# Decoding float64 weights inside an expert pass: raw pieces in resident buffers, half-steps spread over four expert slots

## The chip, the cores and the metric

The kernel runs on one core of one Trainium2 chip. The metric is device time in microseconds (us); the kernel before takes 666.78 us, the median of 3 runs (662.82 to 666.97).

## What is computed

Attention with pooled queries feeds a mixture of experts (each token goes to one of 8 experts by the argmax of its gate), and that feeds a dense layer. Only the dense layer's weights come as float64.

```python
q_pool = q.reshape(B, H, S // 2, 2, D).mean(axis=3)
attn = softmax(scale * q_pool @ k.T);  x = attn @ v              # 1152 tokens x 512
e_idx = argmax(x @ w_gate)
for e in range(8):                                                # w1[e] 512x1024, w2[e] 1024x512
    ye = np.maximum(x[e_idx == e] @ w1[e], 0.0) @ w2[e]
    out[e_idx == e] = gate_w * eom * ye
h = out @ w_in;  g = h * tanh(softplus(h));  return g @ w_out     # w_in, w_out float64
```

## The kernel before

There are three stages in a row. Attention and the routing take roughly the first 280 us, the experts run until 437 us, and the dense layer (tiles zps, u, n, l, gh, gl, ops) takes the rest. TensorE multiplies in float32 with operands split in two: an ACT copy makes the high part (names ending in h), a subtraction on DVE or POOL the low part (names ending in l), and three matmuls a product (lines 1012 to 1014).

**The float64 weights.** They are 32 pieces of 128 x 512 numbers. `load_raw` (from line 508) loads the raw 512 KB of a piece into a tile wraw; `decode` (from line 528) turns it into float32 in the resident tiles `wd[0]` to `wd[15]`, two pieces to a tile, in two half-steps. Half-step 0 has `ACT dm<-wraw` (absolute value of the high word, line 91) and on DVE two operations that make ds (sign and low bits, lines 100 and 97). Half-step 1 has three operations on DVE: two on dm (clamp, shift) and one that writes wd. `raw_ahead` keeps at most two pieces loaded that are not decoded. Pieces 0 to 21 are decoded in the attention stage; pieces 22 to 31 in the expert stage, where the load is issued from ACT's queue (line 513), ACT works in order, and an issue waits there until the buffer is free.

**The expert pass.** Eight slots run one after the other, each one expert of a given size. This text numbers them 0 to 7. Wide slots: 0 and 3 (three blocks of 128 tokens) and 5 (two blocks), ten steps each. Narrow slots: 1 (128 tokens) and 2, 4, 6, 7 (64 tokens), six steps each. One counter q runs over all steps: slot 0 has q 0 to 9, slot 1 q 10 to 15, slot 2 q 16 to 21, slot 3 q 22 to 31, slot 4 q 32 to 37, slot 5 q 38 to 47.

In step i of a wide slot, TensorE makes one block of hidden units (hps, for i under 8) and adds hidden block i - 2 to the output (yp). Between the two stand `ACT hh<-hps` and `DVE hl<-hps,hh`; two hps buffers exist, so a block of hps waits for the hl of two blocks before. Weights (tiles wt, 1 MB each, four to an expert, five buffers) are loaded by SP in order as buffers come free; ACT makes w1h and w2h, DVE w2l and the first three w1l, POOL the other w1l. Slot 1 has the same split for its second product; the 64-token slots multiply in plain float32 and need only ACT (hr, hn). The block of tokens of the next wide slot is prepared in the narrow slot before it (xh on ACT, xl on DVE).

**Where decoding stands in the pass.** The loop over q (from line 1271) calls, after the matmuls and splits of a step, as many half-steps as the table DECS gives. Before, the table has a row for each wide slot, and a step counts from q = 8 on:

```python
DECS = [[0] * 8 + [1, 2], [2, 1] * 5, [2] + [0] * 9]    # slots 0, 3, 5: 3, 15 and 2 half-steps
```

At q = 7 the routing's memory on the right side of SBUF is given up (the last DMA from it is `gbuf<-gt`, the gates' 4.5 KB, issued by ACT), the pool `dq` is opened in it (two wraw, two dm, one ds), and the first two raw loads are issued. When piece 31 is decoded (q = 38), the pool is closed, and `split_hi` (ACT wh, 1024 wide) and `split_lo` (DVE wl or wd) of the dense layer's first four weight tiles run in every second step from there on.

Of the kernel before, what the change touches and what calls it, by code (L numbers as in the profile page):

```python
# [9 lines left out]
F32 = mybir.dt.float32  # L10
F32R = mybir.dt.float32r
F16 = mybir.dt.float16
I32 = mybir.dt.int32
# [7 lines left out]
P = 128  # L21
# [63 lines left out]
def kernel(ctx, tc, cst, qt, kt, v, wgo, w1, w2, wio, out):  # L85
# [48 lines left out]
    wd = [cp.tile([P, 1024], F32, name="wd", bufs=16) for f in range(16)]  # L134
# [8 lines left out]
    ap = astack.enter_context(tc.tile_pool(name="ap", bufs=1, side="right"))  # L143
# [38 lines left out]
    DEC_M = 32  # L182
# [39 lines left out]
    KC = 384  # L222
# [280 lines left out]

    dq, wq = [], []
    wraw, dmt, dst_ = {}, {}, {}

    def load_raw(i, pool):
        f, c = divmod(i, 2)
        if pool is ap and i % 2:
            wraw[i] = wd[12].bitcast(I32).rearrange("p (a b) -> p a b", b=2)  # L510
        else:
            wraw[i] = pool.tile([P, 512, 2], I32, name="wraw", bufs=1 if pool is ap else 2)
        (SP if pool is ap else A).dma_start(out=wraw[i].rearrange("p a b -> p (a b)"), in_=wio[f, :, 512 * c:512 * (c + 1)].bitcast(I32))

    def decode_abs(pool, i=None):
        early = i is None
        if early:
            i = dec[0] + (dec[0] in dmt)
        if i not in dmt and i in wraw and now[0] - since.get(i, 0) >= (3 if early else 0):
            m = dmt[i] = pool.tile([P, 512], F32, name="dm", bufs=2)  # L520
            act(m, wraw[i][:, :, 1].bitcast(F32), AF.Abs)

    clamped = set()
# [6 lines left out]
    def decode(i, part, pool):  # L530
        f, c = divmod(i, 2)
        lo, hi = wraw[i][:, :, 0], wraw[i][:, :, 1]
        dst = wd[f][:, 512 * c:512 * (c + 1)]
        decode_abs(pool, i)
        if part == 0:
            s = dst_[i] = wd[15][:, KC:KC + 512].bitcast(I32) if pool is ap else pool.tile([P, 512], I32, name="ds", bufs=1)
            ts(V, s, hi, -0x80000000, ALU.bitwise_and)
            stt(s, lo, 29, s, ALU.logical_shift_right, ALU.bitwise_or)
        else:
            s, m = dst_[i], dmt[i]  # L540
            mi = m.bitcast(I32)
            decode_clamp(V, i)
            ts(V, mi, mi, 3, ALU.logical_shift_left, 0x40000000, ALU.bitwise_xor)
            stt(dst.bitcast(I32), mi, 0x7FFFFFFF, s, ALU.bitwise_and, ALU.bitwise_or)
# [149 lines left out]
    def raw_ahead(pool, end):  # L694
        while dec[2] < min(dec[0] + 2, end):
            load_raw(dec[2], pool)
            since[dec[2]] = now[0]
            dec[2] += 1

    def decode_step(pool, end):  # L700
        if dec[0] >= dec[2]:
            return
        decode(dec[0], dec[1], pool)
        dec[1] += 1
        if dec[1] == 2:
            dec[0], dec[1] = dec[0] + 1, 0
# [515 lines left out]
    NPRE = 4  # L1222
# [19 lines left out]
    LATE = 1  # L1242
    XGB = 4

    DECS = [[0] * 8 + [1, 2], [2, 1] * 5, [2] + [0] * 9]
    RQ = 2
    slots = []
    for pos_ in order:
# [31 lines left out]
    for q, (n_, i, _, main, w_, _) in enumerate(flat):  # L1280
        if i == 0:
            used += len(slots[n_][1])
            if n_ + 1 < len(slots):
                load_w(slots[n_ + 1][0], ej, slots[n_ + 1][0])
        if q + 2 < len(flat):
            flat[q + 2][2]()
        if gnext < min(used + 4, len(allc)):
            gather(*allc[gnext])
            gnext += 1
        for f in xpre.pop(-q - 1, ()):  # L1290
            f()
        main()
        if q + 2 < len(flat):
            flat[q + 2][5]()
        if q == RQ:
            routing_rest()
            over = routing_over()
        if RQ < q <= RQ + 4:
            oi = next(over)
        if q == RQ + 5:  # L1300
            routing_oix(oi)
            T.transpose(pr[:TT, P:2 * P], gsc, ident)
            gt_ = rt("gt", [P])
            act(gt_[:TT], pr[:TT, P:2 * P])
            A.dma_start(out=gbuf.rearrange("(t p) o -> t (p o)", p=P), in_=gt_[:TT])
            rstack.close()
            fstack = ExitStack()
            fp.append(fstack.enter_context(tc.tile_pool(name="fps", bufs=1, space=PSUM, side="right", reuse_waits="tile")))
            dstack = ExitStack()
            dq.append(dstack.enter_context(tc.tile_pool(name="dq", bufs=1, side="right", reuse_waits="tile")))  # L1310
            raw_ahead(dq[0], DEC_M)
        if w_ and q > RQ + 5:
            for _ in range(DECS[slots[n_][0]][i]):
                decode_step(dq[0], DEC_M)
            raw_ahead(dq[0], DEC_M)
        if dec[0] == DEC_M and dq and not wq:
            dstack.close()
            wq.append(ctx.enter_context(tc.tile_pool(name="wq", bufs=1, side="right", reuse_waits="tile")))
            q0 = q
        elif wq and (q - q0) % 2 == 0 and len(ws2) < NPRE:  # L1320
            f = len(ws2)
            split_hi(0, f)
            split_lo(0, f)
# [268 lines left out]
```

## Time and profile before

| | us |
|---|---|
| median of 3 runs (lowest, highest) | 666.78 (662.82, 666.97) |
| the profiled execution's own time | 667.41 |
| its span, first to last instruction | 665.3 |
| TensorE busy in the span | 624.4 |
| VectorE (DVE) busy | 482.9 |
| ScalarE (ACT) busy | 398.8 |
| GpSimd (POOL) busy | 256.5 |

The rows of the trace are from the profiled execution, and their times count from the start of its span. A row of the timeline gives start, duration, engine, line and operation (out<-in), how many were merged, and in brackets how long the engine sat idle before it and what ended that. "L1012" is line 1012 of the kernel before.

### The profile page before, as it was taken

Reading aid. Unit: us, or ns where it says so; the run is one execution under the profiler, and the core shown is the slowest. Engines: PE = TensorE matmul, PEld = TensorE weight load, DVE = VectorE, ACT = ScalarE, POOL = GpSimd, SP = SyncE. Lnnn points to the kernel's source line nnn. Section 1 sums busy time; section 2 is a strip of 40 time slices with the busy share of each in tenths; the row PEclk is TensorE's granted clock in tenths of the full one; section 3 lists DMA queues with packets and bytes.
Section 4 is the critical chain, followed back from the end, with each engine's and each line's share of the span. In section 5 each row is a group of like instructions: output and inputs, shape, how many; then the busy total and the mean of one; then the engine's idle time right before and its main releaser. Section 6 shows DMA issues by size and latency. Waiting matters only on the chain.

```text
span 665.3 us, 11329 instructions
## 1 busy us (share of the span) xinstructions
PE 624.4 (94%) x4122; PEld 502.0 (75%) x4122; DVE 482.9 (73%) x992; ACT 398.8 (60%) x842; POOL 256.5 (39%) x237
## 2 busy tenths in 40 slices
PE   7899999999999999599899989988999999999995
PEld 4667778777777766388669858677888999999993
DVE  4557797978887787566539947229999796888764
ACT  7588888888888664242445464336665544556442
POOL 6555647374656232341215132112222232324221
PEclk8699999999999999699899998989999999999999
DMA  6857564365452231584898795820000110001001
GB/s 242 294 135 230 163 183 123 107 183 170 102 174 63 89 115 52 166 337 156 303 352 287 274 326 186 286 102 0 2 0 1 48 48 1 1 7 42 1 0 53
DMA packets 27410, 89.90 MB, mean 135 GB/s; under 512 B 2886, under 2 KB 7631, under 8 KB 23250
## 3 DMA queue, kind: packets, MB, share of 16 engines
q1 hardware_dynamic: 22320, 75.07, 32.7%
q0 software_dynamic: 3568, 8.79, 5.7%
q10 hardware_dynamic: 1458, 5.25, 2.3%
q8 instruction: 34, 0.56, 0.3%
q14 instruction: 30, 0.25, 0.1%
HBM read 79.65 MB, written 9.97 MB: 135 GB/s over the span
## 4 chain that ended last, share of the span: by engine, by line
PE 36%; DVE 8%; issue 4%; DMA 1%; ACT 1%; POOL 0%; DVEq 0%; ACTq 0%; POOLq 0%
PE ops L1439 10%; PE zps L1013 4%; PE zps L1012 4%; PE zps L1014 4%; PE hps L1162 2%; DVE l L97 2%; DVE n L97 2%; PE yp L1013 2%; PE yp L1012 2%; PE yp L1014 2%; PE yp L1033 2%; PE hps L1012 1%; PE hps L1014 1%; PE hps L1013 1%; DMA wt<-in_w 1%
## 5 line engine op out<-in xcount | busy, mean ns | idle before, releaser
L100 POOL TENSOR_SCALAR u<-u 128x384 f32<-128x384 f32 x48 | 59.7, 1243 | 150.3 <-ACT u L91 121.3
L91 ACT ACTIVATE pt<-sc 128x320 f32<-128x320 f32 (+1 forms) x198 | 87.9, 490 | 12.9 <-PE sc L322 10.2
L341 PE MATMUL pv<-pt,vt 128*64 128x288 f32 x576 | 75.6, 411 | 0.0
L103 DVE TENSOR_REDUCE Mp<-mx 128x1 f32<-128x384 f32 x72 | 40.1, 556 | 42.8 <-PE mx L237 37.7
L324 PE MATMUL sc<-qs,at 128*128 128x320 f32 (+1 forms) x264 | 68.8, 305 | 0.0
L322 PE MATMUL sc<-qb,Bt 66*128 66x320 f32 (+1 forms) x264 | 67.7, 301 | 0.0
L1012 PE MATMUL zps<-yh,wh 128*128 128x384 f32 x188 | 64.4, 342 | 1.7 <-DVE n L97 1.7
L1014 PE MATMUL zps<-yl,wh 128*128 128x384 f32 x188 | 63.6, 338 | 0.0
L1013 PE MATMUL zps<-yh,wd 128*128 128x384 f32 x180 | 61.2, 340 | 0.0
L1439 PE MATMUL ops<-wh,gl 128*128 128x512 f32 x144 | 57.8, 404 | 2.9 <-DVE gl L94 2.4
L341 PEld LDWEIGHTS pv<-pt,vt 128*64 128x64 f32 x576 | 39.0, 137 | 28.5 <-issue 5.2
L1439 PE MATMUL ops<-wh,gh 128*128 128x512 f32 x144 | 56.9, 395 | 0.2 <-ACT gh L91 0.2
L1439 PE MATMUL ops<-wd,gh 128*128 128x512 f32 x135 | 53.3, 395 | 0.0
L100 POOL TENSOR_SCALAR dm<-dm 128x512 f32<-128x512 f32 x21 | 41.5, 1978 | 23.1 <-ACT dm L91 23.0
L94 POOL TENSOR_TENSOR Bt<-kd,at 64x576 fp32r<-64x576 f32 x32 | 46.1, 1452 | 7.1 <-ACT at L91 7.0
L324 PEld LDWEIGHTS sc<-qs,at 128*128 128x128 f32 x264 | 47.4, 194 | 1.3 <-issue 1.0
L322 PEld LDWEIGHTS sc<-qb,Bt 66*128 66x128 f32 x264 | 46.5, 194 | 0.1
L91 ACT ACTIVATE l<-n,two 128x384 f32<-128x384 f32 x48 | 29.5, 615 | 24.9 <-DVE n L97 24.9
L91 ACT ACTIVATE u<-zps 128x384 f32<-128x384 f32 x48 | 23.2, 484 | 33.4 <-PE zps L1014 30.7
L97 DVE SCALAR_TENSOR_TENSOR l<-n,r 128x384 f32<-128x384 f32 x48 | 26.6, 554 | 20.1 <-ACT r L91 20.1
L1012 PEld LDWEIGHTS zps<-yh,wh 128*128 128x128 f32 x188 | 35.6, 190 | 3.7 <-ACT r L91 2.0
L237 PE MATMUL mx<-at,qs 128*128 128x384 f32 x120 | 36.4, 371 | 2.0 <-DVE Mp L103 1.0
(314 smaller groups left out, 1604.9 us busy)
## 6 DMA issues: line engine op xcount, KB each, us to landing
wt<-in_w SPq DMA_DIRECT2D x32, 1024.0 KB, 7.4
kd<-in_kt SPq DMA_DIRECT2D x16, 576.0 KB, 8.2
wraw<-in_wio SPq DMA_DIRECT2D x11, 512.0 KB, 6.1
wd<-in_wio SPq DMA_DIRECT2D x11, 512.0 KB, 4.0
wraw<-in_wio ACTq DMA_DIRECT2D x10, 512.0 KB, 6.0
vt<-in_v SPq DMA_DIRECT2D x8, 576.0 KB, 5.8
tq<-in_qt SPq DMA_DIRECT2D x12, 288.0 KB, 5.5
tq<-in_qt POOLq DMA_DIRECT2D x12, 288.0 KB, 6.8
```

The lines of the kernel that those rows point to most:

```text
L91: A.activation(out=out, in_=in_, func=func, **kw)
L94: eng.tensor_tensor(out=out, in0=a, in1=b, op=op)
L97: V.scalar_tensor_tensor(out=out, in0=a, scalar=s, in1=b, op0=op0, op1=op1)
L100: eng.tensor_scalar(out=out, in0=a, scalar1=s1, scalar2=s2, op0=op0, op1=op1)
L103: V.tensor_reduce(out=out, in_=in_, axis=AX.X, op=op)
L322: mm(o, lhsT=Bt[(2 * p + h) % NBL][:66, ks], rhs=QB[p, h][:66, qs_], start=False, stop=last_, skip_group_check=not (first and last_))
L324: mm(o, lhsT=At[p, h][:, ks], rhs=QS[p, h][:, qs_], start=first, stop=False, skip_group_check=not (first and last_))
L341: mm(pvt[p][f][64 * h:64 * h + 64, :HQ], lhsT=vt[p][:, t, h, :], rhs=Pt[p, t][:, h, f * HQ:(f + 1) * HQ], start=t == 0, stop=t == KT - 1, ...
L1012: mm(out_, lhsT=a, rhs=c, start=first, stop=False)
L1013: mm(out_, lhsT=b_, rhs=c, start=False, stop=False)
L1014: mm(out_, lhsT=a, rhs=d, start=False, stop=last_)
L1439: mm(opt[b_, j], lhsT=(g_, g_, gl_)[i], rhs=(wo, wl_, wo)[i], start=f == 0 and i == 0, stop=f == NF - 1 and i == 2)
```

## The change

Four edits. First, raw loads start at q = 3 instead of q = 7: until the pool is opened, pieces go into `wd[14]` and `wd[15]` (tiles that are decoded last and are free by then), with `wd[13]` for the two work tiles. So pieces 22, 23 and 24 are loaded there. Second, DECS is a table over slots 0 to 3: 5 half-steps in slot 0 (q 5 to 9), 2 in slot 1 (q 14, 15), 3 in slot 2 (q 16 to 18), 10 in slot 3 (one in each step), none in slot 5. Third, the pool `dq` is opened at q = 7 as before, but its first raw load (piece 25) is issued at q = 8. Fourth, `split_hi` and `split_lo` of the first four dense tiles run at q 39, 41, 43 and 45 instead of 40, 42, 44 and 46.

```diff
+    scratch = object()
     def load_raw(i, pool):
         f, c = divmod(i, 2)
-        if pool is ap and i % 2:
+        if pool is scratch:
+            wraw[i] = wd[14 + i % 2].bitcast(I32).rearrange("p (a b) -> p a b", b=2)
+        elif pool is ap and i % 2:
...
-            m = dmt[i] = pool.tile([P, 512], F32, name="dm", bufs=2)
+            m = dmt[i] = wd[13][:, 512:] if pool is scratch else pool.tile([P, 512], F32, name="dm", bufs=2)
...
-            s = dst_[i] = wd[15][:, KC:KC + 512].bitcast(I32) if pool is ap else pool.tile([P, 512], I32, name="ds", bufs=1)
+            if pool is scratch:
+                s = wd[13][:, :512].bitcast(I32)
...
-    DECS = [[0] * 8 + [1, 2], [2, 1] * 5, [2] + [0] * 9]
+    DECS = [[0] * 5 + [1] * 5, [0] * 4 + [1, 1], [1] * 3 + [0] * 3, [1] * 10]
...
-            raw_ahead(dq[0], DEC_M)
-        if w_ and q > RQ + 5:
-            for _ in range(DECS[slots[n_][0]][i]):
-                decode_step(dq[0], DEC_M)
-            raw_ahead(dq[0], DEC_M)
+        if q > RQ and n_ < len(DECS):
+            dp_ = dq[0] if dq else scratch
+            for _ in range(DECS[n_][i]):
+                decode_step(dp_, DEC_M)
+            raw_ahead(dp_, DEC_M)
...
-            q0 = q
-        elif wq and (q - q0) % 2 == 0 and len(ws2) < NPRE:
+        elif wq and n_ == 5 and i % 2 and len(ws2) < NPRE:
```

TensorE's, POOL's and SP's instructions keep their order. ACT's and DVE's move, as the following rows show; "waits" names what an instruction waits for by semaphore, and a DMA's eight semaphores are DMAHW0 to DMAHW7.

ACT, from the gates' store at q = 7 (end of slot 0) to the first relu of slot 1 (hh 128x512), before:

```order
L91 ACTIVATE gt<-pr 9x128 [waits PE_49]
L1305 DMA gbuf<-gt 9x128 [waits Activation_49]
L513 DMA wraw<-in_wio 128x1024 [waits DVE_49] x2
L91 ACTIVATE dm<-wraw 128x512 [waits DMAHW3_49,DMAHW2_49,DVE_49]
L91 ACTIVATE w2h<-wt 128x512 [waits DMAHW7_49]
L91 ACTIVATE w2h<-wt 128x512
L91 ACTIVATE y<-yp 128x512 [waits PE_49] x3
L91 ACTIVATE dm<-wraw 128x512 [waits DMAHW4_49]
L513 DMA wraw<-in_wio 128x1024 [waits DMAHW6_49,DVE_49,Activation_49]
L91 ACTIVATE w2h<-wt 128x512 x2
L91 ACTIVATE hh<-hps 128x512 [waits PE_49]
```

The same place in the changed kernel:

```order
L91 ACTIVATE gt<-pr 9x128 [waits PE_49]
L1314 DMA gbuf<-gt 9x128 [waits DMAHW5_49,Activation_49]
L91 ACTIVATE dm<-wd 128x512 [waits DMAHW1_49]
L516 DMA wraw<-in_wio 128x1024 [waits DMAHW6_49,DMAHW5_49,DVE_49]
L91 ACTIVATE w2h<-wt 128x512 [waits DMAHW0_49]
L91 ACTIVATE w2h<-wt 128x512
L91 ACTIVATE y<-yp 128x512 [waits PE_49] x3
L91 ACTIVATE dm<-wd 128x512 [waits DMAHW3_49]
L91 ACTIVATE w2h<-wt 128x512 x2
L91 ACTIVATE hh<-hps 128x512 [waits PE_49]
```

The two loads and the absolute value that waits for the first of them are gone from this place; what is left is one load (piece 25), which waits for DMAHW5, the semaphore of the gates' store right before it.

DVE, in the first two steps of slot 5 (hl 128x256 is the low part of its hidden blocks), before:

```order
L97 SCALAR_TENSOR_TENSOR hl<-hps,hh 128x256
L94 TENSOR_TENSOR w2l<-wt,w2h 128x512
L100 TENSOR_SCALAR ds<-wraw 128x512
L97 SCALAR_TENSOR_TENSOR ds<-wraw,ds 128x512
L100 TENSOR_SCALAR dm<-dm 128x512 x2
L97 SCALAR_TENSOR_TENSOR wd<-dm,ds 128x512
L97 SCALAR_TENSOR_TENSOR hl<-hps,hh 128x256
L94 TENSOR_TENSOR w2l<-wt,w2h 128x512
```

The same place in the changed kernel:

```order
L97 SCALAR_TENSOR_TENSOR hl<-hps,hh 128x256
L94 TENSOR_TENSOR w2l<-wt,w2h 128x512
L97 SCALAR_TENSOR_TENSOR hl<-hps,hh 128x256
L94 TENSOR_TENSOR w2l<-wt,w2h 128x512
L94 TENSOR_TENSOR wl_4882<-wd,wh 128x1024
```

The five operations of piece 31 no longer stand between the first and the second hl; the first dense split (wl) comes one step earlier.

DVE, from the last splits of slot 1 through slot 2 to the first w1l of slot 3, in the changed kernel:

```order
L94 TENSOR_TENSOR w2l<-wt,w2h 128x512 x2
L100 TENSOR_SCALAR dm<-dm 128x512 x2
L97 SCALAR_TENSOR_TENSOR wd<-dm,ds 128x512
L100 TENSOR_SCALAR ds<-wraw 128x512
L97 SCALAR_TENSOR_TENSOR ds<-wraw,ds 128x512
L100 TENSOR_SCALAR dm<-dm 128x512 x2
L97 SCALAR_TENSOR_TENSOR wd<-dm,ds 128x512
L94 TENSOR_TENSOR xl<-xps,xh 128x4x128
L100 TENSOR_SCALAR ds<-wraw 128x512
L97 SCALAR_TENSOR_TENSOR ds<-wraw,ds 128x512
L94 TENSOR_TENSOR xl<-yb_4295,xh 128x4x128
L100 TENSOR_SCALAR dm<-dm 128x512 x2
```

Before, DVE has there only the splits w2l, the three xl and then w1l; five half-steps (pieces 24 to 26) are new between them.

## Rows read from the trace of the kernel before

**Rows 1.** The page: busy us of each engine over the span.
```profile
PE 624.4 (94%) x4122; PEld 502.0 (75%) x4122; DVE 482.9 (73%) x992; ACT 398.8 (60%) x842; POOL 256.5 (39%) x237
```

**Rows 2.** Stretches: length, busy of PE, PEld, DVE, ACT, POOL, clock, DMA share, GB/s.
```profile
299.00:306.00 7.00, 7.00 (x37) 6.35 (x36) 6.59 (x21) 2.00 (x4) 2.35 (x2) 1.00 0.80 300
306.00:314.00 8.00, 8.00 (x50) 6.87 (x49) 4.75 (x17) 2.62 (x5) 0.00 (x0) 1.00 0.00 0
327.00:350.00 23.00, 21.51 (x128) 14.89 (x129) 9.83 (x17) 10.74 (x23) 6.16 (x6) 0.93 1.00 353
...
329.10:332.50 3.40, 3.40 (x10) 2.26 (x11) 1.55 (x3) 1.74 (x3) 0.77 (x1) 0.51 0.98 402
...
346.50:380.70 34.20, 34.20 (x176) 30.40 (x176) 31.12 (x52) 17.44 (x34) 11.78 (x10) 1.00 0.82 287
...
400.80:404.20 3.40, 3.40 (x15) 3.20 (x15) 3.40 (x6) 0.96 (x3) 0.47 (x1) 0.51 0.29 120
```

**Rows 3.** Timeline of PE in slot 1 and at the start of slot 5.
```profile
317.96 7.30 PE L1201 MATMUL hps<-xn,wt 128*128 128x128 f32 x64
327.19 0.50 PE L1012 MATMUL yp<-w2h,hh 128*128 128x512 f32 x1 [1.93 <-ACT hh L91]
328.99 0.67 PE L1013 MATMUL yp<-w2h,hl 128*128 128x512 f32 x1 [1.30 <-DVE hl L97]
...
400.52 0.39 PE L1012 MATMUL hps<-xh,w1h 128*128 128x256 f32 x1 [3.76 <-DVE hl L97]
```

**Rows 4.** Timeline of ACT, end of slot 0 and start of slot 1.
```profile
314.35 0.55 ACTq L1305 DMA_DIRECT2D gbuf<-gt  x1
314.94 0.98 ACTq L513 DMA_DIRECT2D wraw<-in_wio  x2
321.88 0.69 ACT L91 ACTIVATE dm<-wraw 128x512 f32<-128x512 f32 x1 [7.57 <-DMA wraw<-in_wio]
322.47 1.14 ACT L91 ACTIVATE w2h<-wt 128x512 fp32r<-128x512 f32 x2
...
323.51 1.55 ACT L91 ACTIVATE y<-yp 128x512 f32<-128x512 f32 x3
324.94 0.68 ACT L91 ACTIVATE dm<-wraw 128x512 f32<-128x512 f32 x1
325.51 1.15 ACT L91 ACTIVATE w2h<-wt 128x512 fp32r<-128x512 f32 x2
326.55 0.60 ACT L91 ACTIVATE hh<-hps 128x512 fp32r<-128x512 f32 x1
```

**Rows 5.** Timeline of DVE at the start of slot 5.
```profile
394.83 0.69 DVE L94 TENSOR_TENSOR w2l<-wt,w2h 128x512 fp32r<-128x512 f32 x1 [2.13 <-ACT w2h L91]
395.44 0.42 DVE L100 TENSOR_SCALAR ds<-wraw 128x512 int32<-128x512 int32 x1
...
396.50 2.90 DVE L100 TENSOR_SCALAR dm<-dm 128x512 f32<-128x512 f32 x2
...
400.05 0.42 DVE L97 SCALAR_TENSOR_TENSOR hl<-hps,hh 128x256 fp32r<-128x256 f32 x1
```

**Rows 6.** Timeline of DVE: last hidden block of slot 0.
```profile
311.90 0.56 DVE L97 SCALAR_TENSOR_TENSOR hl<-hps,hh 128x384 fp32r<-128x384 f32 x1 [2.31 <-ACT hh L91]
```

**Rows 7.** Decode operations by tile: count, ns min/median/max, first and last start; landing of raw pieces.
```profile
L100 DVE TENSOR_SCALAR ds<-wraw x10: 414/424/437, 321.8 to 395.4; 128x512 int32<-128x512 int32 x10
L97 DVE SCALAR_TENSOR_TENSOR wd<-dm,ds x10: 691/693/1664, 325.2 to 399.4; 128x512 int32<-128x512 int32 x10
...
DMA to landing us min/median/max: 3.7/6.0/7.0
```

**Rows 8.** Timelines of DVE before slot 3 and of ACT in its first step.
```profile
339.72 0.69 DVE L94 TENSOR_TENSOR xl<-xps,xh 128x512 fp32r<-128x512 f32 x1 [4.70 <-ACT xh L91]
342.70 0.69 DVE L94 TENSOR_TENSOR xl<-yb,xh 128x512 fp32r<-128x512 f32 x1 [2.29 <-ACT xh L91]
...
349.31 0.63 ACT L91 ACTIVATE w2h<-wt 128x512 fp32r<-128x512 f32 x1
```

More of the change, by code (lines that the diff above doesn't have):

```diff
@@ L535, in decode @@
         if part == 0:
-            s = dst_[i] = wd[15][:, KC:KC + 512].bitcast(I32) if pool is ap else pool.tile([P, 512], I32, name="ds", bufs=1)
+            if pool is scratch:
+                s = wd[13][:, :512].bitcast(I32)
+            elif pool is ap:
+                s = wd[15][:, KC:KC + 512].bitcast(I32)
+            else:
+                s = pool.tile([P, 512], I32, name="ds", bufs=1)
+            dst_[i] = s
             ts(V, s, hi, -0x80000000, ALU.bitwise_and)
```

## The prediction

> **What bounds the kernel now.** Read the page first: TensorE is busy for 624.4 us of a span of 665.3, 94% [rows 1]. So a change that adds and removes no matmul can win only TensorE's idle time and the time in which its clock is low. Next, read the expert stage stretch by stretch, because only that stage is touched, and look for TensorE's idle times and the clock. In slot 3, where 15 of the 20 half-steps stand, TensorE is busy for 34.20 of 34.20 us although DVE is at 31.12 [rows 2]: decoding is hidden there, and taking five half-steps away wins nothing. The idle time stands at two other places [rows 3]. At the start of slot 1's second product TensorE waits 1.93 us for hh and then 1.30 us for hl; in slot 5 it waits 3.76 us for hl. Each is followed by a stretch with the clock at 0.51, that is at 1.2 GHz instead of 2.4: 329.1 to 332.5 and 400.8 to 404.2, 3.40 us each, with TensorE busy all the time [rows 2].
>
> Then go back along the engine that was waited for. In slot 1 it is ACT [rows 4]: hh starts at 326.55, although its matmuls run from 317.96 on [rows 3], because ACT stood still for 7.57 us for the first raw piece, issued at 314.94 in the same queue, and afterwards had a row of w2h, y, dm and w2h to work off. In slot 5 it is DVE [rows 5]: between w2l (394.83) and hl (400.05) stand the five operations of piece 31, and two of them, the dm pair, take 2.90 us there against about 0.85 at two medians of 0.424 [rows 7] (the ds row, the nearest of the same form).
>
> **The change part by part.**
>
> *Slot 1's stall.* Pieces 22 to 24 now come into wd[14] and wd[15] from q = 3 on, four steps ahead of the gates' store at 314.35 [rows 4]. Slot 3's ten steps take 34.20 us, so a wide step is about 3.4 us and the first issue falls near 300; the DMA engines have nothing to do from 306 to 314 (share 0.00) [rows 2]. With a landing of 6.0 us at the median and 7.0 at most [rows 7], pieces 22 and 23 are there by 308, near q = 5, and ACT's absolute values hardly wait. What goes: 1.93 + 1.30 us idle, and half of the 3.40 us at a clock of 0.51, 0.49 x 3.40 = 1.67. Together 4.90 us.
>
> What is late next: ACT's new wait. The load of piece 25 waits for the gates' store (DMAHW5 in the order), because its buffer lies where the gates lay. Behind it on ACT stand w2h, w2h, the three y, one dm, two w2h and hh, and TensorE waits for that hh and the hl after it. Their work is 1.14 + 1.55 + 0.68 + 1.15 = 4.52 us, plus 0.60 for hh [rows 4]. TensorE wants hh at 317.96 + 7.30 = 325.26 [rows 3], so ACT must be free by 325.26 - 5.12 = 320.1. The store is issued at 314.35 and takes 0.55 [rows 4]; no row shows when it lands. Bounds from the nearest rows, raw loads of 512 KB: 3.7 us after the issue at the least and 7.0 at the most [rows 7], so ACT is free between 318.1 and 321.4. At the early end nothing is lost; at the late end hh is 1.3 us late, and if the clock falls again, most of the 4.90 stays. Since the store has 4.5 KB and not 512, I take the early end.
>
> The Trainium skill ("DMA: Bandwidth & Descriptors", section "Anatomy of one DMA — SWDGE (gpsimd) path") gives a DMA, measured there on those that GpSimd issues, a fixed cost of about 2.0 us. By that, as an estimate for this store, ACT would be free near 317, well before it matters; no run here shows it, and the sum does not use it.
>
> *Slot 5's stall.* Its two half-steps go. hl then follows w2l directly: hh permitting it starts near 395.5 instead of 400.05, and TensorE, which was out of work at 400.52 - 3.76 = 396.76 [rows 3], finds its hps buffer free. What goes: 3.76 + 1.67 = 5.43 us. What is late next is POOL's w1l and the first dense split, which now comes one step earlier: DVE's wl stands behind the second w2l, so it does not delay the second hl. I cost it at nothing.
>
> *Slot 0.* It gets five half-steps instead of three, from q = 5 on instead of q = 8. A half-step 0 takes 0.42 + 0.69 = 1.1 us of DVE and a half-step 1 takes 0.42 + 0.42 + 0.69 = 1.5 [rows 7]. DVE is full from 299 to 306 (6.59 of 7.00) with routing work, then loosens (4.75 of 8.00) [rows 2]. By q = 7 two half-steps, 2.6 us, are put ahead of the last hl, which before waited 2.31 us for ACT [rows 6]. So that hl is 0.3 us late, and the output product takes it two steps later. Nothing is lost. If DVE were late by one half-step more, 1.5 us, it would still be within those two steps.
>
> *Slots 1 and 2.* Five half-steps, 1.5 + 1.1 + 1.5 + 1.1 + 1.5 = 6.7 us of DVE, stand between the last w2l of slot 1 and the w1l that slot 3 starts with. Before, DVE sat idle there for 4.70 and 2.29 us ahead of two of the xl alone [rows 8], and it was busy for 9.83 of 23.00 us from 327 to 350 [rows 2]. They fit by their sum, but piece 26 is issued only about one landing (6.0 us) before its first half-step. Bounds: nothing, or its lateness of up to 7.0 - 6.0 = 1.0 us and one half-step of 1.5 on w1l. I take 0.6 for this, and 0.4 for hl of slot 1's second half behind two w2l: 1.0 us of small new waits, an estimate.
>
> *Slot 3 and the totals.* Ten half-steps instead of 15; TensorE was full before and stays so. The number of half-steps, 20, and of raw bytes is unchanged.
>
> *Sum.* 4.90 + 5.43 - 1.0 = 9.3 us. The profiled execution's own time is 667.41 (span 665.3 and 2.1 around it): 658.1. It stands 0.63 above the median of the runs; on the median the sum gives 657.5. I take 657.8, between them.
>
> **The rivals.**
>
> *A. ACT stands behind the gates' store.* Place: piece 25's load at q = 8. For it: the order puts that wait on ACT, and in the trace ACT's 7.57 us wait at the same place led to the stall [rows 4]. Against it: 4.5 KB, and the DMA engines are nearly empty until 314. It decides from 320.1 us on. Slot 1's stall then stays and only slot 5's goes: 657.8 + 4.9 = 662.7 us.
>
> *B. The decoding in slot 2 delays slot 3.* Place: xl and w1l on DVE. For it: 6.7 us of new work on an in-order engine, one part of which waits for a raw piece. Against it: the idle times of rows 8. It decides if piece 26 lands more than 1 us late. Price: some 2.5 us idle and 1.67 of clock: 657.8 + 4.2 = 662.0 us.
>
> *C. The weight stream is the bound there, and the time gets longer.* Place: 327 to 350, where the DMA share is 1.00 at 353 GB/s [rows 2]. Pieces 26 to 28 (three times 0.524 MB, 1.57 MB) are now loaded in it, 1.57 MB / 353 GB/s = 4.5 us. If SP's weights were just in time, TensorE could not start slot 3 sooner, so slot 1's 4.90 us are won and lost again, and slot 3 idles 4.5 us with 1.67 of clock behind: 667.41 + 4.5 + 1.67 - 5.43 = 668.1 us, slower than before. For it: the share. Against it: ACT's w2h of slot 3 (349.31) waited for no DMA [rows 8], the loads follow the release of buffers, which come sooner when slots 1 and 2 do, and pieces 22 to 24 leave the stretch from 315 on.
>
> The Trainium skill speaks for C ("DMA: Bandwidth & Descriptors", section "Issuing engines are not separate DMA queues"): DMAs issued from ACT and from SP run on the same 16 engines and interleave, so ACT's queue is no second path. By that rule the pieces cost the weights their full 4.5 us wherever the engines are full. The trace agrees on the sharing: with share 1.00 the stretch moved 353 GB/s for both queues together.
>
> **How the numbers follow.** Forecast 0.62, A 0.18, B 0.12, C 0.08. Faster by over 1% means under 660.1 us (1%, 6.7 us, is about what a measurement of this kernel tells from no change). The forecast lies under it but for a few hundredths, and a part of A and B lies there too when they cost half: 0.64. Slower by over 1% (above 673.5) needs C with a second such place: 0.04. The rest, 0.32, is within 1%. The range: at the low end both stalls go without new waits, 667.41 - 10.33 = 657.1, less what slot 5's weights gain by piece 31's absence, 1.49 us at 353 GB/s: 655.5. At the high end A and B: 663.3. C and two rivals at once are left out.
>
> **What would show it.** In the changed profile: no idle time of TensorE for hh at slot 1's second product and a clock of 1.00 through slots 1 and 2; ACT's dm<-wd without a wait; the raw load at q = 8 held less than 5 us; the second hl of slot 5 right behind w2l and no idle time over 1 us there. The prediction is wrong if TensorE waits anew at the start of slot 3 (B: for w1l or xl; C: for w2h after a DMA), if ACT is held at q = 8 beyond the end of slot 1's first product (A), or if a clock of 0.51 shows up in slots 1 to 5 at all.

## The result, and the profile after

The changed kernel takes 655.70 us, the median of 4 runs (653.36 to 658.23), beside 666.18 us of the kernel before on the same chip (662.82 to 666.97): a ratio of 0.9866, 95% interval 0.9832 to 0.9900. On another chip, with 6 runs, it was 655.05 us and 0.9835 (0.9797 to 0.9872). The forecast was 657.8, with a range of 655.5 to 663.3: 655.70 lies just inside the low end, and the 655.05 of the other chip just below it. By the medians the gain is 10.5 us on this chip and 10.4 on the other. The profiled execution has a span of 656.1 us, 9.2 less than before; the sum had said 9.3. For this pair of executions the total is thus nearly exact, but its terms are not, as the stages show.

The page of the changed kernel answers to [rows 1]: TensorE lost 4.9 us of busy time with the same 4122 matmuls, so part of the gain is clock.

```profile
PE 619.5 (94%) x4122; PEld 498.1 (76%) x4122; DVE 482.7 (74%) x992; ACT 399.5 (61%) x842; POOL 258.1 (39%) x237
```

Next the stretches of the changed kernel, with the columns of [rows 2]. The first is slot 1 from its first product to slot 2's first hps, the third slot 3 from its first hps to that of slot 4, the fourth slot 5 in the same way, and the last lies in the dense stage.

```profile
318.12:331.45 13.33, 13.33 (x93) 11.71 (x91) 9.00 (x15) 8.00 (x15) 4.33 (x4) 1.00 0.76 282
327.00:350.00 23.00, 20.98 (x139) 15.38 (x136) 14.24 (x26) 10.99 (x23) 3.94 (x4) 1.00 1.01 403
341.46:378.74 37.28, 35.11 (x174) 30.14 (x172) 27.53 (x44) 16.34 (x32) 11.79 (x10) 1.00 0.76 287
388.01:411.30 23.29, 23.29 (x150) 20.66 (x148) 17.05 (x26) 15.76 (x30) 9.60 (x6) 1.00 0.69 254
440.00:446.00 6.00, 4.84 (x28) 4.53 (x26) 5.34 (x8) 3.98 (x8) 3.66 (x3) 1.00 0.00 0
```

The same view of the kernel before, for slots 1, 3 and 5 and for the stretch of the dense stage in which its clock was low:

```profile
317.96:336.52 18.56, 15.33 (x93) 12.71 (x91) 10.17 (x17) 8.54 (x16) 4.58 (x4) 0.91 0.88 309
346.53:380.63 34.10, 34.10 (x175) 30.33 (x173) 31.05 (x52) 17.41 (x34) 11.71 (x10) 1.00 0.82 286
390.13:419.63 29.50, 25.59 (x151) 21.92 (x149) 20.19 (x31) 16.23 (x31) 8.96 (x6) 0.94 0.62 219
445.20:448.60 3.40, 3.40 (x13) 3.40 (x12) 0.00 (x0) 1.37 (x2) 0.79 (x1) 0.50 0.00 0
```

Slot 1 is 5.23 us shorter and slot 5 6.21, both with TensorE busy all the time and a clock of 1.00. Slot 3 is 3.18 us longer: TensorE is busy for 35.11 of 37.28 us, where before it had no idle time. From 327 to 350 the DMA engines are full in both kernels, but they now move 403 GB/s instead of 353.

TensorE's timeline of the changed kernel, beside [rows 3]:

```profile
318.12 7.30 PE L1210 MATMUL hps<-xn,wt 128*128 128x128 f32 x64
325.19 0.48 PE L1021 MATMUL yp<-w2h,hh 128*128 128x512 f32 x1
...
341.46 0.44 PE L1021 MATMUL hps<-xh,w1h 128*128 128x384 f32 x1
350.00 0.50 PE L1021 MATMUL yp<-w2h,hh 128*128 128x512 f32 x1 [2.02 <-ACT w2h L91]
```

In slot 1 the second product now follows the first without a wait. The new wait, 2.02 us for w2h, stands at slot 3's second product. ACT's timeline, beside [rows 4] and [rows 8], shows both places from the other side:

```profile
314.51 0.53 ACTq L1314 DMA_DIRECT2D gbuf<-gt  x1
315.09 0.68 ACT L91 ACTIVATE dm<-wd 128x512 f32<-128x512 f32 x1 [0.61 <-ACT gt L91]
318.56 0.36 ACTq L516 DMA_DIRECT2D wraw<-in_wio  x1
318.97 1.15 ACT L91 ACTIVATE w2h<-wt 128x512 fp32r<-128x512 f32 x2 [3.20 <-DMA gbuf<-gt]
...
323.07 0.61 ACT L91 ACTIVATE hh<-hps 128x512 fp32r<-128x512 f32 x1
...
343.85 0.49 ACT L91 ACTIVATE hh<-hps 128x384 fp32r<-128x384 f32 x1 [0.98 <-PE hps L1023]
349.32 0.63 ACT L91 ACTIVATE w2h<-wt 128x512 fp32r<-128x512 f32 x1 [4.97 <-DMA wt<-in_w]
```

The gates' store holds ACT until 318.56, and hh is still done by 323.68, before TensorE wants it at 325.19. In slot 3 ACT waits 4.97 us for the weights themselves, where before the same w2h (349.31) waited for no DMA [rows 8]. DVE's timeline of the changed kernel, for the last hl of slot 0 and the start of slot 5, beside [rows 6] and [rows 5]:

```profile
312.25 0.55 DVE L97 SCALAR_TENSOR_TENSOR hl<-hps,hh 128x384 fp32r<-128x384 f32 x1
...
390.17 0.42 DVE L97 SCALAR_TENSOR_TENSOR hl<-hps,hh 128x256 fp32r<-128x256 f32 x1
390.69 0.69 DVE L94 TENSOR_TENSOR w2l<-wt,w2h 128x512 fp32r<-128x512 f32 x1
391.61 0.42 DVE L97 SCALAR_TENSOR_TENSOR hl<-hps,hh 128x256 fp32r<-128x256 f32 x1 [0.23 <-ACT hh L91]
```

The 9.2 us, cut at the first hps of each slot and at the first zps of the dense stage:

| part | before | after | difference |
|---|---|---|---|
| up to slot 1 | 317.96 | 318.12 | +0.16 |
| slot 1 | 18.56 | 13.33 | -5.23 |
| slot 2 | 10.01 | 10.01 | 0 |
| slot 3 | 34.10 | 37.28 | +3.18 |
| slot 4 | 9.50 | 9.27 | -0.23 |
| slot 5 | 29.50 | 23.29 | -6.21 |
| slots 6 and 7 to the first zps | 24.38 | 24.92 | +0.54 |
| dense stage | 221.29 | 219.88 | -1.41 |

### The profile page after: what moved, and what is told of

Read it like the earlier page. It is cut to its first block, busy times and chain, and to the rows that moved or that the text cites. A ratio compares the mean times of both kernels' runs of the same rounds, so it can differ in the third digit from the quotient of the medians.

```text
span 656.1 us, 11326 instructions
## 1 busy us (share of the span) xinstructions
PE 619.5 (94%) x4122; PEld 498.1 (76%) x4122; DVE 482.7 (74%) x992; ACT 399.5 (61%) x842; POOL 258.1 (39%) x237
## 4 chain that ended last, share of the span: by engine, by line
PE 72%; DVE 10%; issue 6%; ACT 4%; DMA 3%; POOL 3%; SPq 0%; ACTq 0%; DVEq 0%; POOLq 0%
PE ops L1447 10%; PE pv L341 10%; PE mx L237 5%; PE sc L324 5%; PE sc L322 5%; PE zps L1022 4%; PE zps L1021 4%; PE zps L1023 4%; DMA wt<-in_w 3%; PE pv L373 3%; PE yp L1021 2%; PE yp L1023 2%; PE yp L1022 2%; DVE l L97 2%; DVE n L97 2%
## 5 line engine op out<-in xcount | busy, mean ns | idle before, releaser
L94 DVE TENSOR_TENSOR w2l<-wt,w2h 128x512 fp32r<-128x512 f32 x32 | 28.2, 886 | 14.7 <-ACT w2h L91 14.1
```

Source lines behind the costliest of these rows:

```text
L94: eng.tensor_tensor(out=out, in0=a, in1=b, op=op)
```

## The experiments

The theory after the result: both stalls went as forecast, and rival C, which had been given 0.08, took place beside them: raw pieces 26 to 28 made slot 3's weights late. Against it stood B (decoding on DVE is what delays slot 3), and a further one: that SP can issue these weights only when a buffer comes free. The dense stage's 1.41 us had no theory.

**One part of the change alone: slot 1.** The kernel before, with pieces 22 and 23 loaded early.

```diff
+        if pool is scratch:
+            wraw[i] = wd[14 + i % 2].bitcast(I32).rearrange("p (a b) -> p a b", b=2)
...
+        if q == RQ + 1:
+            raw_ahead(scratch, DEC_M)
```

> The kernel before with the other part alone: pieces 22 and 23 are loaded at q = 3 into wd[14] and wd[15]; every half-step stays where it was, so only piece 24's load stands between slot 1 and slot 3. Theory: slot 1 without idle time of TensorE for hh or hl and without the low clock, from its first product to slot 2's first hps 13.3 us instead of 18.56, and of these 5.2 us at least 4 are kept at slot 4's start, because two raw pieces less stand in the stream than in the changed kernel (where 3.2 of them were lost again in slot 3); slot 5's stall of 3.76 us stays. Time 4 to 5.2 us under before, ratio 0.993. Rival (the weights bound slot 3 in any case: whoever arrives 5 us sooner waits there): idle time of 2 us or more for w2h at slot 3's start, slot 4 starts at most 2 us sooner, time about 2 us under before.

Measured: ratio 0.9929 (0.9903 to 0.9954), median 659.99 against 664.72. The stretches are slots 1, 3 and 5:

```profile
313.61:326.94 13.33, 13.33 (x93) 11.71 (x91) 7.38 (x12) 6.21 (x12) 4.06 (x4) 1.00 0.85 297
336.95:371.06 34.11, 34.11 (x175) 30.34 (x173) 30.49 (x52) 17.27 (x34) 11.19 (x10) 1.00 0.83 294
380.59:410.25 29.66, 25.63 (x151) 21.79 (x149) 20.14 (x31) 16.23 (x31) 9.46 (x6) 0.94 0.58 213
```

Slot 1 gives all 5.23 us, slot 3 keeps them although it starts so much sooner, and slot 5 stalls as before (3.75 us idle for hl, 29.66 us in all). So slot 3's weights are not late merely because TensorE arrives sooner: the full stretch has room for that, if no raw piece is in it.

**The other part alone: slot 5.** The kernel before, with piece 31's two half-steps in slot 3; a second line, not shown, keeps the dense splits at q 40, 42, 44 and 46.

```diff
-    DECS = [[0] * 8 + [1, 2], [2, 1] * 5, [2] + [0] * 9]
+    DECS = [[0] * 8 + [1, 2], [2, 2, 1, 2, 2, 1, 2, 2, 1, 2], [0] * 10]
```

> The kernel before with one part of the change alone: the two half-steps of slot 5 go into slot 3 (17 there instead of 15), slot 1's raw loads stay as they were, and the first four dense splits stay at q 40, 42, 44 and 46. Theory (piece 31's five operations on DVE made the stall of slot 5): no idle time of TensorE over 1 us at slot 5's second hl, no stretch at a clock of 0.51 there, and from the first hps of slot 5 to the first of slot 6 some 23.3 us as in the changed kernel instead of 29.5; the stall of slot 1 (1.93 and 1.30 us) stays. Time 5.4 to 6.2 us under the kernel before, ratio 0.991. Rival (the stall comes from the weights: w2l before it waited 2.13 us for w2h, and that for its stream): the stall moves to w2l and shrinks by less than 2 us, time at most 2 us under before, ratio 0.997 or more.

Measured: ratio 0.9941 (0.9910 to 0.9972), some 3.9 us instead of 5.4 to 6.2. Slot 5 and, ahead of it, slot 4:

```profile
389.80:413.09 23.29, 23.29 (x150) 20.66 (x148) 16.71 (x26) 15.79 (x30) 9.33 (x6) 1.00 0.68 238
376.31:389.80 13.49, 10.91 (x77) 6.07 (x77) 7.21 (x13) 4.94 (x11) 3.54 (x4) 0.87 0.88 313
```

Slot 5 gained its whole 6.21 us, and slot 4, 9.50 before, lost 3.99. ACT's timeline of this kernel at that place tells why:

```profile
380.70 0.67 ACT L91 ACTIVATE dm<-wraw 128x512 f32<-128x512 f32 x1 [3.69 <-DMA wraw<-in_wio]
381.27 0.37 ACT L91 ACTIVATE hr<-hps 128x256 f32<-128x256 f32 x1
```

With 17 half-steps in ten steps, piece 31's absolute value comes before its load has landed, and hr, which TensorE needs, is queued behind it: TensorE idles 2.58 us, and the clock is at 0.50 from 383 to 386. It is slot 1's stall once more, made by an experiment in another slot. Two things stay open. In this one trace slot 1's first product to the first zps takes 124.91 us, only 1.14 less than before, so the trace does not account for the whole 3.9 us. And the weights of slot 5 had 4 us more to land here, so this kernel cannot tell piece 31's operations from its bytes.

**Piece 31 put back.** The changed kernel, with only those two half-steps returned to slot 5.

```diff
-    DECS = [[0] * 5 + [1] * 5, [0] * 4 + [1, 1], [1] * 3 + [0] * 3, [1] * 10]
+    DECS = [[0] * 5 + [1] * 5, [0] * 4 + [1, 1], [1] * 3 + [0] * 3, [1] * 8 + [0] * 2, [0] * 6, [2] + [0] * 9]
```

> The changed kernel with the two half-steps of piece 31 taken out of slot 3 and put back into the first step of slot 5; the dense splits stay at q 39, 41, 43 and 45. Theory (the five operations on DVE between w2l and hl are the whole stall of slot 5): TensorE idles 3.5 to 4 us for hl in slot 5, a stretch at a clock of 0.51 follows, the dm pair takes well over its 0.88 us there because POOL's w1l run beside it, slot 5 takes 29.3 to 29.7 us instead of 23.29, and the time is about 6.2 us longer than that of the changed kernel. Rival (the new place of the dense splits, or the earlier weights, gained a part): idle time of 2.5 us or less, no low clock, slot 5 at most 26.5 us, time at most 3.2 us longer.

Measured: ratio 0.9943 (0.9917 to 0.9968), where the changed kernel had 0.9866 and 0.9835. Slot 5 takes 27.52 us, between the two expectations, with 2.44 us idle for hl and a clock of 0.51 from 394.4 to 397.8. DVE's timeline:

```profile
388.01 0.69 DVE L94 TENSOR_TENSOR w2l<-wt,w2h 128x512 fp32r<-128x512 f32 x1
...
389.68 1.99 DVE L100 TENSOR_SCALAR dm<-dm 128x512 f32<-128x512 f32 x2
391.71 1.64 DVE L97 SCALAR_TENSOR_TENSOR wd<-dm,ds 128x512 int32<-128x512 int32 x1
393.27 0.41 DVE L97 SCALAR_TENSOR_TENSOR hl<-hps,hh 128x256 fp32r<-128x256 f32 x1
```

The five operations cost 4.23 us of the 6.21 (27.52 - 23.29). The w2l ahead of them is not late here, whereas in the kernel before it started 2.13 us late [rows 5], behind a w2h for which ACT had waited 1.92 us for the weights; piece 31's bytes had run beside that stream until 384.6. That leaves the other 2 us. The five operations themselves took as long in both kernels, 4.61 and 4.65 us from the first start to that of hl; what differs is when w2l starts after slot 5's first hps, 4.70 us in the kernel before and 2.68 here. So slot 5's stall had two causes: piece 31's operations on DVE, which this run shows, and weights that came late. That piece 31's bytes made them late is read from the rows and not shown: in this kernel slot 3 also took 37.03 us instead of 34.10, which may have given the weights some 3 us more to land, and no run took those bytes away alone.

**Fewer raw pieces in the full stretch, first way.** The changed kernel, with slot 2's three half-steps moved into slot 3, so that pieces 27 and 28 are loaded later.

```diff
-    DECS = [[0] * 5 + [1] * 5, [0] * 4 + [1, 1], [1] * 3 + [0] * 3, [1] * 10]
+    DECS = [[0] * 5 + [1] * 5, [0] * 4 + [1, 1], [0] * 6, [2, 1, 1, 2, 1, 1, 2, 1, 1, 1]]
```

> The changed kernel with the three half-steps of slot 2 moved into slot 3 (13 there): the loads of pieces 27 and 28 (1.05 MB) then come after slot 3 has begun, and only piece 26 is left among the weights from 327 to 350. Theory (raw pieces made slot 3's weights late, rival C in part): 1.05 MB at 403 GB/s are 2.6 us, so ACT's wait of 4.97 us for slot 3's first w2h falls to about 2.4, TensorE's 2.02 us there vanishes, slot 4 starts 2 to 3 us sooner than 378.7, and the time is 2 to 3 us under the changed kernel. Rival 1 (slot 3's w2 weights come late because SP could issue them only when a buffer came free): the waits stay within 0.5 us and the time is that of the changed kernel. Rival 2 (B: decoding on DVE in slot 2 delayed slot 3): DVE's w1l and xl of slot 3 move forward, but the w2h wait for its DMA does not shrink.

Measured: ratio 0.9869 (0.9830 to 0.9907), no different from the changed kernel's. ACT's first w2h of slot 3 and TensorE's wait there:

```profile
342.41 0.63 ACT L91 ACTIVATE w2h<-wt 128x512 fp32r<-128x512 f32 x1 [1.75 <-DMA wt<-in_w]
...
347.99 0.45 PE L1021 MATMUL hps<-xh,w1h 128*128 128x384 f32 x1 [1.60 <-DVE hl L97]
```

The wait for the weights fell from 4.97 to 1.75 us, and TensorE no longer waits for w2h. This speaks against the buffers, and against B only in part, since the half-steps left slot 2 together with the loads. But two half-steps on DVE now stand in slot 3's first step, and TensorE waits 1.60 us for the hl behind them. Slot 3 takes 35.97 us instead of 37.28. This run took away one wait and set another, so its time decides nothing.

**Fewer raw pieces, second way.** The half-steps stay; only the loads move, into the time in which the DMA engines have room: 24 goes with 22 and 23, 25 to 27 follow at q 6, 8 and 9, and 28 waits until slot 3; the two work tiles move to wd[12].

```diff
-            wraw[i] = wd[14 + i % 2].bitcast(I32).rearrange("p (a b) -> p a b", b=2)
+            wraw[i] = wd[{22: 14, 23: 15, 24: 13, 25: 14, 26: 15}[i]].bitcast(I32).rearrange("p (a b) -> p a b", b=2)
...
-            raw_ahead(dp_, DEC_M)
+            for i_ in {3: (22, 23, 24), 6: (25,), 8: (26,), 9: (27,)}.get(q, ()):
+                load_raw(i_, scratch if i_ < 27 else dp_)
+                since[i_] = now[0]
+                dec[2] = i_ + 1
+            if q >= 22:
+                raw_ahead(dp_, DEC_M)
```

> The changed kernel with its half-steps in the same places, but every raw piece except 28 loaded before the stretch in which the DMA engines are full: 22, 23 and 24 at q = 3 (wd[14], wd[15], wd[13]; the two work tiles in wd[12]), 25 at q = 6, 26 at q = 8, 27 at q = 9, and 28 only at q = 22. Theory: as for the kernel without decoding in slot 2, and a little more: 1.57 MB less in the stretch, 3.9 us at 403 GB/s, so slot 3 starts its second product without waiting for w2h, slot 4 starts near 375.6 instead of 378.7, and the time is about 3 us under the changed kernel. Rival 1 (release of buffers on SP, not the raw pieces): slot 3 as before, time that of the changed kernel. Rival 2 (the pieces loaded from 318 to 327 now delay the weights of slots 1 and 2): a new wait for w2h or hr there of 1 to 2 us, and the time within 1 us of the changed kernel.

Measured: ratio 0.9827 (0.9770 to 0.9885), median 653.95 against 664.72. Slot 3:

```profile
341.63:375.74 34.11, 34.11 (x175) 30.43 (x173) 27.56 (x43) 16.33 (x32) 11.93 (x10) 1.00 0.78 289
```

Slot 3 is back at 34.11 us, with w2h waiting 0.80 us and TensorE not at all. The half-steps stand where the change put them, so B is out. From slot 1's first product to the first zps this kernel takes 114.47 us, the changed one 118.10, the one before 126.05. The interval of its time overlaps that of the changed kernel; the runs side by side, below, tell the two apart.

**More raw pieces.** The changed kernel with two loads more, which nothing reads.

```diff
             raw_ahead(dp_, DEC_M)
+            if q == 16:
+                for e in (14, 15):
+                    A.dma_start(out=wd[e].bitcast(I32), in_=wio[e, :, :512].bitcast(I32))
```

> The changed kernel with two loads more from ACT at q = 16 in slot 2: raw pieces of 0.524 MB that nothing reads go into wd[14] and wd[15], 1.05 MB in addition to the three pieces of the changed kernel in the full stretch. Theory (each byte of raw pieces in that stretch makes slot 3's weights later by its own time): 1.05 MB at 403 GB/s are 2.6 us, so ACT's wait for slot 3's first w2h grows from 4.97 to about 7.5 us, TensorE's from 2.02 to about 4.6, a stretch at a low clock follows it (as after the idle times of 3.2 and 3.8 us in the kernel before), slot 3 takes 39.9 to 41.5 us instead of 37.28, and the time is 2.6 to 4.3 us longer than that of the changed kernel. Rival (SP's late issue of these weights sets the wait, not the bytes beside them): waits within 0.7 us of the changed kernel's, time the same.

Measured: ratio 0.9879 (0.9829 to 0.9929), no different from the changed kernel's. The theory missed. Slot 3 takes 39.11 us, less than the 39.9 expected at the least, and ACT's wait is 5.31 us and TensorE's 2.35, only 0.34 and 0.33 more, which is what the rival had said; the rest of slot 3's length is a clock of 0.50 from 350.0 to 353.4. The view of the DMA queues, cut to 20 us that begin 9 us after slot 1's first product, says where the bytes went. Its columns are packets, MB and share of the 16 engines; q1 is SP's queue with the weights, q10 ACT's with the raw pieces. The third line of each is SP's five weight loads of that stretch, with the median us from issue to landing at its end. This is the kernel with two more, then the changed one, then that with the loads moved early (no q10 there, so two lines):

```profile
q1 hardware_dynamic: 710, 5.20, 65.0%
q10 hardware_dynamic: 474, 1.75, 22.3%
wt<-in_w SPq DMA_DIRECT2D x5, 1024.0 KB, 13.9
```

```profile
q1 hardware_dynamic: 742, 5.43, 67.4%
q10 hardware_dynamic: 431, 1.57, 20.0%
wt<-in_w SPq DMA_DIRECT2D x5, 1024.0 KB, 12.6
```

```profile
q1 hardware_dynamic: 961, 7.04, 88.1%
wt<-in_w SPq DMA_DIRECT2D x5, 1024.0 KB, 9.1
```

| kernel | weights, MB | raw, MB | sum | w2h's wait | TensorE's wait | slot 3 |
|---|---|---|---|---|---|---|
| slot 1's part alone | 7.23 | 0 | 7.23 | 0 | 0 | 34.11 |
| loads moved early | 7.04 | 0 | 7.04 | 0.80 | 0 | 34.11 |
| half-steps moved to slot 3 | 6.50 | 0.52 | 7.02 | 1.75 | 1.60 (for hl) | 35.97 |
| changed kernel | 5.43 | 1.57 | 7.00 | 4.97 | 2.02 | 37.28 |
| two loads more | 5.20 | 1.75 | 6.95 | 5.31 | 2.35 | 39.11 |

What raw pieces move, the weights do not, nearly byte for byte: the sum stays between 6.95 and 7.23 MB (a third queue, GpSimd's, moved 0.49 to 1.05 MB besides). But of the 2.62 MB issued on ACT's queue in the last kernel only 1.75 got through; the rest stood in that queue (median landing 17.5 us, against 9.4 in the changed kernel), and hardly hurt the weights. Cut into stretches of 2 us, ACT's queue moved 0.10 to 0.29 MB in each from 332 to 346 in the changed kernel, and 0.14 to 0.30 from 330 to 348 in the one with two loads more: it had work all that time in both, and its rate did not grow with what stood in it.

SP's own timeline settles its rival. Counted from slot 1's first product, SP issues those five weight loads at 11.85, 15.32, 18.31, 21.73 and 23.46 us in the changed kernel, and within 0.01 us of these in the one with the loads moved early and in the one with two loads more. Issued at the same moments, they took 12.6, 9.1 and 13.9 us to land. So it was not a late issue that made them late, but what shared the engines with them.

The Trainium skill ("DMA: Bandwidth & Descriptors", section "Queues, rings and completion order") says that a DMA engine takes turns between the queues that have work, a packet at a time. By that a queue with a backlog gets its turns and no more, however long the backlog; the rows agree, 1.57 and 1.75 MB, though no view shows the single turns.

**The gates' wait.** The changed kernel with piece 25's load in a buffer that is free of it.

```diff
-        if pool is scratch:
+        if pool is scratch or i == 25:
             wraw[i] = wd[14 + i % 2].bitcast(I32).rearrange("p (a b) -> p a b", b=2)
```

> The changed kernel with piece 25's raw load put into wd[15] (free after piece 23) instead of the buffer that lies where the gates lay, so the load no longer waits for the gates' store. Theory (that wait, 3.20 us on ACT, is hidden, because hh is wanted only at 325.2): ACT does its two w2h of slot 1 within about 1.5 us after the absolute value of piece 23, 2 to 3 us sooner than in the changed kernel against the start of slot 1, and TensorE gains nothing from it: from slot 1's first product to slot 2's first hps 13.3 us as in the changed kernel (within 0.2), time within 1 us of it after allowing for the attention stage. Rival (rival A in part: the wait costs something further on, through the later w2h and y): slots 1 and 2 together get shorter by 0.5 us or more than their 23.34 us in the changed kernel (318.12 to 341.46).

Measured, in one execution (656.18 us), on ACT's timeline: the two w2h come 0.80 us behind the absolute value, and hh starts 3.77 us after slot 1's first product instead of 4.95.

```profile
313.05 0.67 ACT L91 ACTIVATE dm<-wd 128x512 f32<-128x512 f32 x1 [0.61 <-ACT gt L91]
314.12 0.36 ACTq L516 DMA_DIRECT2D wd<-in_wio  x1
314.52 1.15 ACT L91 ACTIVATE w2h<-wt 128x512 fp32r<-128x512 f32 x2 [0.80 <-DVE dm L100]
...
319.85 0.60 ACT L91 ACTIVATE hh<-hps 128x512 fp32r<-128x512 f32 x1 [1.12 <-issue]
```

Slots 1 and 2 take 23.36 us, in the changed kernel 23.34: in these two slots the wait is hidden in full, and rival A cost nothing. Slot 3 took 36.62 us here instead of 37.28, with TensorE waiting 1.35 us for w2h instead of 2.02. Whether that comes of piece 25's earlier load or only of the execution stays open with one run.

**The kernel before, a second trace.**

> The kernel before, unchanged, for a second trace. Open is whether the stretch at half clock at 445.2 to 448.6 in the dense stage, which the changed kernel did not show, belongs to the kernel before. Theory 1 (it belongs to it): again a clock of about 0.51 for some 3.4 us shortly after the first zps, span and time as before. Theory 2 (it comes and goes between executions of one kernel, like the one from 22 to 32 us): it is absent, and of the 9.2 us by which the spans differ 1.4 are no effect of the change. In both cases the stalls of slots 1 and 5 stand as before: 1.9, 1.3 and 3.8 us.

Measured: span 659.0 us. The first stretch is slot 1, the second the place in the dense stage:

```profile
316.24:332.77 16.53, 13.88 (x93) 11.78 (x92) 10.17 (x17) 8.58 (x16) 4.59 (x4) 1.00 0.88 314
...
440.50:444.00 3.50, 3.50 (x22) 3.50 (x22) 0.45 (x1) 1.60 (x3) 1.19 (x1) 1.00 0.02 5
```

The dense stage has no low clock here: theory 2 holds, and 1.4 of the 9.2 us belong to the execution. In slot 1, too, the clock stayed at 1.00 after waits of 1.36 and 1.29 us; the slot took 2.03 us less than in the first trace. Slot 5's stall was there again, 3.64 us, and the slot took 28.75 us instead of 29.50. So the profiled price of both stalls depends on the execution: 3.20 or 5.23 us for slot 1, 5.46 or 6.21 for slot 5.

**The changed kernel and the best one, side by side.**

> The changed kernel, unchanged, on the same chip as the next run: for a direct comparison, and to see whether its new wait at slot 3's start is steady. Theory (raw pieces 26 to 28 share the full DMA engines with slot 3's weights in each execution): ACT waits 4 to 5.3 us for slot 3's first w2h, TensorE 1.3 to 2.1 us, slot 3 takes 36.5 to 37.5 us; ratio to the kernel before 0.985 to 0.99. Rival (the wait was an accident of one execution): slot 3 takes 34.1 to 34.5 us as in the kernel before.

> The kernel with all raw pieces but 28 loaded before the full stretch, unchanged, for a tighter interval beside the changed kernel. Theory: slot 3 again 34.1 us, no idle time of TensorE over 0.5 us from slot 1 to slot 7, and the time about 3 us (2.5 to 3.7) under the changed kernel of the same chip, ratio to the kernel before 0.981 to 0.985. Rival (what slot 3 wins is lost further on): ratio within 0.002 of the changed kernel's.

Measured on one chip: 655.05 us, 0.9835 (0.9797 to 0.9872), for the changed kernel, and 650.94 us, 0.9781 (0.9743 to 0.9820), for the one with the loads moved early; before 665.48. The medians differ by 4.1 us, a little over the 2.5 to 3.7 expected. The changed kernel's slot 3, and its dense stage:

```profile
338.96:377.42 38.46, 36.27 (x174) 31.72 (x173) 27.80 (x44) 16.33 (x32) 11.81 (x10) 0.96 0.76 281
434.50:438.00 3.50, 3.34 (x11) 3.37 (x12) 0.61 (x2) 0.67 (x1) 0.00 (x0) 0.55 0.00 0
```

The kernel with the loads moved early, from slot 2 to the end of slot 5:

```profile
328.34:405.02 76.68, 76.68 (x478) 62.41 (x477) 55.26 (x88) 42.53 (x83) 27.22 (x21) 1.00 0.79 291
```

The wait in slot 3 is steady (5.14 us on ACT, 2.18 on TensorE), and here a low clock followed it, so that the slot took more than the 36.5 to 37.5 us expected. In the other kernel TensorE is busy for 76.68 of 76.68 us. Both ratios came out below what was expected, by 0.0015 and 0.0029.

## Why the prediction was right, and where it was not

*Slot 1's stall, 4.90.* Right: 5.23 us, and shown alone by the kernel with that part only. Of the 4.90, the 1.67 of clock is no fixed price: the second trace of before has the stall without it, and there the slot is only 3.20 us longer than in the changed kernel.

*The gates' wait.* Right: it came, was 3.20 us on ACT, ended inside the bounds of 318.1 to 321.4 and was hidden. That the early end was taken turned out well, but the argument for it, 4.5 KB instead of 512, was poor: the load behind the store was issued 4.05 us after it (318.56 - 314.51), within the 3.7 to 7.0 us of a 512 KB load. The estimate by the Trainium skill ("DMA: Bandwidth & Descriptors", section "Anatomy of one DMA — SWDGE (gpsimd) path"), free near 317, was too early here.

*Slot 5's stall, 5.43.* Right in the mechanism, mis-sized by 0.8: 6.21. Left out were 0.66 us ahead of the stall, where the slot's first output products ran late behind weights that landed late. "Its two half-steps go. hl then follows w2l directly" held to the row.

*Slot 0.* Right: the last hl came at 312.25, 0.35 us later than before (0.19 if counted to slot 1's first product; forecast 0.3), and nobody waited for it.

*Slots 1 and 2, 1.0 us of small new waits, and slot 3, where "TensorE was full before and stays so".* This is the step that failed. It looked at DVE, found room there, and gave a DMA landing late one half-step. There was no new wait in slots 1 and 2; the cost was 3.18 us, stood in slot 3 and lay on the weights. The prediction had named a new wait of TensorE at the start of slot 3, for w2h after a DMA, as a sign that it is wrong, and by that sign it was, although its time came out. Rival C had named the place, the cause and the row to look at, and was dismissed by three arguments. "ACT's w2h of slot 3 (349.31) waited for no DMA" was read in a kernel whose TensorE came 5 us later. That the loads follow the release of buffers was true and did not help, since issued loads then shared the engines. That pieces 22 to 24 leave the stretch was true mainly of 315 to 327: from 327 to 347 ACT's queue had moved 0.34 MB before, and moved 1.57 MB now. (The 353 GB/s, read as those of two queues, were of three: SP's, ACT's, and GpSimd's with 1.30 MB.) C's price was near for the weights and too high for TensorE. ACT's w2h came 7.86 us after slot 3's first hps, and 3.68 with the loads moved early: 4.18 us late, against C's 4.5. But TensorE, with three blocks of hidden units to multiply first, wanted it only 6.5 us after that hps, and lost 3.18 us: the wait of 2.02 and small waits behind it. Nor does each further piece cost its time: two more made w2h wait 0.34 us longer. So the time went down and not up. The Trainium skill's rule ("DMA: Bandwidth & Descriptors", section "Issuing engines are not separate DMA queues") agrees with the runs: the sum of both queues stays at 6.95 to 7.23 MB in 20 us in the five kernels of the table, however it is divided.

*B.* Not so: slot 3 starts without a wait for w1l or xl, and in the kernel with the loads moved early, whose half-steps stay in slot 2, it takes 34.11 us.

*The sum.* That 9.3 us came out as 9.2 is luck, by errors that cancel: the stalls gave 1.1 more than forecast, slots 3 and 4 cost 1.95 more than the 1.0, slots 6 and 7 lost 0.54 unforeseen (0.41 of it a wait for weights in slot 7), and the clock of the dense stage, which the change does not touch, gave 1.41 (0.16 is the start of slot 1). It holds for this pair of executions alone. From slot 1's first product to the first zps the first traces differ by 7.95 us (126.05 and 118.10) and the second ones by 4.08 (123.12 and 119.04), mainly because the clock fell after other waits; and the 10.5 and 10.4 us of the medians are in no pair of traces accounted for term by term. Luck, too, is the place at the range's low end: it was meant for both stalls going without new waits, and there was a new wait. The high end, 663.3, follows from no sum: A gives 662.7 and B 662.0.

## What to carry to other kernels

Before a load is moved into a stretch in which the DMA engines are full, ask what lands there just in time once the stall ahead of it is gone: that a transfer caused no wait in the old trace says nothing of a kernel that reaches it 5 us sooner. Place such loads where the share of the DMA engines is low, and price them by the bytes that the urgent queue does not move, not by the bytes issued. On an engine that works in order, a step that TensorE does not need belongs behind the steps that it waits for, above all if that step waits for a transfer. Slot 1's stall and the one that an experiment made anew were such a wait; in slot 5 it was plain work, five operations ahead of hl.

## What the runs showed of the hardware

The same 128x512 pair of DVE operations (dm, in place) took 0.88 us where POOL was idle and 1.85 to 2.90 us where POOL's w1l ran beside it: in the kernel before at 396.50, 2.90 us [rows 5]. The same kernel at a place where POOL was idle, and POOL's row beside the 2.90 us:

```profile
371.07 0.88 DVE L100 TENSOR_SCALAR dm<-dm 128x512 f32<-128x512 f32 x2
...
395.97 3.16 POOL L94 TENSOR_TENSOR w1l<-wt,w1h 128x512 fp32r<-128x512 f32 x2 [3.69 <-ACT w1h L91]
```

The Trainium skill tells of this ("SBUF — State Buffer", section "Who interferes with whom"): VectorE and GpSimd have one pair of ports in common, and the second to come waits until the first is done. The rows agree, and about 2 us of slot 5's stall are of that origin by them; no run took POOL's work away there.

TensorE's clock did not answer evenly to idle times of about 2 us. After the 2.02 us in slot 3 of the changed kernel it stayed at 1.00, in its second trace 2.18 us were followed by 0.50, and the 2.23 us before the first zps, the same in every kernel, were followed by a low clock in some executions and not in others. A further stretch at 0.50, from 22 to 32 us in the attention stage, was whole in the profiled executions of before and after, and absent in those of the kernels with one part alone, which reached slot 1 at 313.61 and 313.39 instead of 317.96 (the second had a shorter low stretch of its own, from 14 to 18 us). How much of the spread between runs comes of this is not shown, since only one execution of each run was profiled. But 4 us at the start of slot 1 are more than slot 3's loss: such a loss is seen in the trace, and in the times only with several runs.
